# Four early weight pieces issued from GpSimd, their cast and subtraction on ticks of their own, the fifth after the sparse stage

## The chip, the core and the metric

The kernel runs on one core of one Trainium2 chip. TensorE (PE) multiplies, VectorE (DVE), ScalarE (ACT) and GpSimd (POOL) do the elementwise work, SyncE (SP) issues most DMAs. The metric is the device time of one execution in microseconds; lower is better. Before the change it is 521.82 us, the median of three runs from 516.04 to 524.46 us. Two per cent of that is 10.4 us.

## What is computed

Block-sparse attention over 4 batches, 8 heads, 768 positions and 64 dimensions (a position sees its neighbour blocks of 32, the first and the last block, and three sampled blocks; the first and last block see all), then a mixture of 8 experts with the best one chosen for each of 3072 tokens:

```python
scores = np.where(mask, scale * np.matmul(q, k.transpose(0, 1, 3, 2)), -1e9)
attn = softmax(scores); x = (attn @ v) as [3072, 512]
logits = x @ w_gate + modality_bias[modality_id]
e_idx = np.argmax(logits, axis=1)
for e in range(E):                       # 8 experts
    mask = e_idx == e
    h = np.maximum(x[mask] @ w1[e], 0.0)  # 512 x 1024
    out[mask] = gate_w[mask, None] * (h @ w2[e])  # 1024 x 512
```

## The kernel before

**Attention.** A list of items is worked off in one hand-written order for all engines (`manual_schedule`). An item of the sparse stage is a pair of query blocks, one of two batches; four items make a group m, 11 groups make a half, and two halves make groups 0 to 21. At each step t the loop runs the operations O, X, T, S, M, G, V, A, Y, W for items that lag behind t by fixed amounts. For a group: SP loads queries (L148), the values of its own sampled blocks (L525, six loads of 128 KB) and two more rows (L499, L500); POOL copies shared keys (L469, L473, L485) and shared values (L507); PE makes scores (L537), DVE masks them and takes the maximum (L545), ACT takes the exponent (L553), PE transposes (L562), ACT copies back (L567), PE weighs the values (L584 with the shared values, L593 with the group's own). Then the rows are turned (L600), gated (L610) and written to `x_d` (L335). Buffers for values alternate between two slots (`vbuf`, slots 7 and 8).

**Experts.** A group of experts is 256 tokens of one expert. Its weights come in 8 pieces of 512 KB: pieces 0 to 3 are `w1` (L720), 4 to 7 are `w2` (L724). A piece n is loaded into a staging buffer (`fetch`), cast to float32r by ACT (`split_high`, L731: the high part), and its remainder is taken by a subtraction (`split_low`, L737: the low part), on POOL in four quarters for the pieces in `POOL_SPLITS` (1, 2, 4, 7 ...), on DVE otherwise. A product then takes three matmuls: high by high, high by the low part of the tokens, low by high (L785 to L787 for the first layer `up`, L800 to L802 for the second, `down`). Between the layers ACT takes the relu (L792) and DVE the remainder (L793).

**The early groups.** Two expert groups are chosen before all tokens are routed. `choose` writes the expert's number to `grp_e` (L1061), and starts `early_groups`, which is stepped along with the last part of the sparse stage. Each of its ticks is one step t of the attention loop. `TICKS` and `load` decide what happens at a tick: at tick 0 pieces 0 and 1 are fetched; at tick 6 piece 0 is split and piece 2 fetched; at tick 9 piece 1 is split and piece 3 fetched; at tick 12 piece 2 is split and piece 4 fetched. `fetch` reads the expert's number from `grp_e` into a register of SP (L706) and issues the DMA on SP, in line with the value loads of the sparse stage. When the sparse stage has issued its last own-value matmuls (`tail[0]`), `load(10, 5)` splits pieces 3 and 4 and fetches up to piece 9, and the 96 matmuls of the first layer follow, bank by bank: four banks, each with four c and two f. After each bank comes its relu. The second layer calls `load` before each f from the table `DOWN0`.

The staging buffers of pieces 0 to 7 of the first group are 0, 1, 0, 1, 0, 1, 0, 2 of `stg`; 0 and 1 lie in slot 4, and 2, 3 and 4 lie in slot 7, which the sparse stage uses for values until group 20 is done.

Of the kernel before, what the change touches and what calls it, by code (L numbers as in the profile page):

```python
# [26 lines left out]
E = 8  # L27
# [52 lines left out]
EVAC_DVE = ()  # L80
POOL_SPLITS = (1, 2, 4, 7, 15, 16, 21)

TICKS = (6, 9, 12)
DOWN0 = ((9, 5), (9, 7), (14, 7), (12, 9), (13, 9), (13, 9), (17, 9), (15, 10))
UP1 = ((13, 8), (13, 14), (17, 15), (20, 15))
DOWN1 = ((16, 17), (17, 16), (17, 17), (23, 18), (21, 17), (23, 18), (23, 19), (22, 19))
# [3 lines left out]
def attention_moe(ctx, tc, kD, qD, qH, v0, v1, blocks, modality, w_gate, bias, w1, w2, out):  # L90
    nc = tc.nc
# [32 lines left out]
    with ExitStack() as actx:  # L124
# [5 lines left out]
        def bank():  # L130
            return psum.tile([P, 512], F32, name="bank")
# [525 lines left out]
        stg, wh, wl, xg, xh, xl, hh, hl, og, xq = [], [], [], [], [], [], [], [], [], []  # L657
# [42 lines left out]
        experts = {}  # L700
        out_t = dram_disjoint_views(out, 2)

        def expert(g):
            if g not in experts:
                src = grp_e[g] if g < NEAR else grp[:, g:g + 1]
                experts[g] = nc.sync.value_load(src[0:1, :], min_val=0, max_val=E - 1)  # L706
            return experts[g]

        def staged(n):
            return stg[(0, 1, 0, 1, 0, 1, 0, 2)[n] if n < 8 else n % NSTG]  # L710

        def fetch(n):
            g, c = divmod(n, 8)
            e = expert(g)
            if c < 4:
                if g < FIRST_Q:
                    src = w1[bass.ds(e, 1), c * P:(c + 1) * P, :].rearrange("e p f -> p (e f)")
                else:
                    src = w1[bass.ds(e, 1)].rearrange("e (p c) f -> c p (e f)", c=4)[c]
                nc.sync.dma_start(staged(n), src)  # L720
            else:
                c -= 4
                src = w2[bass.ds(e, 1), 2 * c * P:(2 * c + 2) * P, :].rearrange("e (k p) f -> p (e k) f", p=P)
                nc.sync.dma_start(staged(n).rearrange("p (k f) -> p k f", k=2), src)  # L724

        def split(n):
            split_high(n)
# [2 lines left out]
        def split_high(n):  # L730
            nc.scalar.copy(wh[n % NRING], staged(n))  # L731
# [49 lines left out]
        def up(g, c, f, o):  # L781
            h, l = wh[(8 * g + c) % NRING], wl[(8 * g + c) % NRING]
            o = o[:, (f % 2) * GT:(f % 2 + 1) * GT]
            fs = slice(f * P, (f + 1) * P)
            nc.tensor.matmul(o, lhsT=h[:, fs], rhs=xh[g % 2][:, c, :], start=c == 0 and f % 2 == 0, stop=False)  # L785
            nc.tensor.matmul(o, lhsT=h[:, fs], rhs=xl[g % 2][:, c, :], start=False, stop=False)  # L786
            nc.tensor.matmul(o, lhsT=l[:, fs], rhs=xh[g % 2][:, c, :], start=False, stop=c == 3 and f % 2 == 1)  # L787

        def relu(k, o):
            rh = hh[0][:, 2 * k:2 * k + 2, :].rearrange("p a b -> p (a b)")  # L790
            rl = hl[k // 2][:, k % 2 * 2:k % 2 * 2 + 2, :].rearrange("p a b -> p (a b)")
            nc.scalar.activation(rh, o, AF.Relu)  # L792
            nc.vector.scalar_tensor_tensor(rl, o, 0.0, rh.bitcast(F32), ALU.max, ALU.subtract)  # L793
# [22 lines left out]
        def early_groups():  # L816
            now = {"fetch": 0, "split": 0, "gather": 0, "column": 0}

            def load(nf, ns):
                while True:  # L820
                    f, p = now["fetch"], now["split"]
                    if p < ns and p < f:
                        split(p)
                        now["split"] += 1
                    elif f < nf and f - NSTG < p and (f < 8 * NEAR or known):
                        fetch(f)
                        now["fetch"] += 1
                    else:
                        return

            def rows(g):
                if now["gather"] == g and ready[g] and (g != 1 or tail[1]):
                    if g == 1:
                        expert_slots(8)
                    gather(g)
                    now["gather"] += 1

            def columns(g):
                for n in range(2):
                    if now["column"] == 2 * g + n and now["gather"] > g:  # L840
                        column(g, n, bank())
                        now["column"] += 1
                        return

            expert_slots(0)
            tick, wait = 0, 0
            while not tail[0]:
                rows(0)
                if now["gather"]:
                    wait += 1  # L850
                    if wait > 4:
                        columns(0)
                p = sum(tick >= x for x in TICKS)
                load(p + 2, p)
                tick += 1
                yield "tick"
            expert_slots(2, 5, 6, 7)
            while now["column"] < 2:
                rows(0)
                columns(0)  # L860
            load(10, 5)
            for k in range(4):
                o = bank()
                for c in range(4):
                    for f in (2 * k, 2 * k + 1):
                        up(0, c, f, o)
                    rows(1)
                    yield
                relu(k, o)
            o = [bank() for _ in range(2)]  # L870
            for f in range(8):
                load(*DOWN0[f])
                for t in range(2):
                    down(0, f, t, o[t])
                    rows(1)
                    yield
                if f in (3, 7):
                    columns(1)
            while not tail[1]:
                yield  # L880
            rows(1)
            for t in range(2):
                give(0, t, o[t])
            while now["column"] < 4:
                columns(1)
            o = [bank() for _ in range(4)]
            for c in range(4):
                load(*UP1[c])
                for f in range(8):
                    up(1, c, f, o[f // 2])  # L890
                    if f % 2:
                        rows(2)
                        yield
            for k in range(4):
                relu(k, o[k])
            o = [bank() for _ in range(2)]
            for f in range(8):
                load(*DOWN1[f])
                for t in range(2):
                    down(1, f, t, o[t])  # L900
                    rows(2)
                    yield
                if f in (5, 6):
                    columns(2)
            for t in range(2):
                give(1, t, o[t])
            while not ready[2]:
                yield
            rows(2)
            load(22, 17)  # L910
            while now["column"] < 6:
                columns(2)
            piece_numbers(bank())
            load(22, 20)
# [537 lines left out]
```

## Time and profile before

| | |
|---|---|
| median of 3 runs | 521.82 us (516.04 to 524.46) |
| the profiled execution | 518.86 us, span of its instructions 517.2 us |
| granted TensorE clock, mean | 0.994 |
| PE busy | 495.8 us (96%) |
| DVE, ACT, POOL busy | 389.9, 339.1, 296.1 us |
| DMA moved | 119.40 MB, 231 GB/s |

The profile is one execution. Times in its views are us from the start of the span. The busy share of an engine over the whole span is a mean over stages with different limits: the dense and sparse attention (to about 227 us), the two early expert groups, and the other expert groups. A row of waits names who ended the waiting; "issue" stands where no semaphore did. A row of the timeline gives start, duration, engine, line, operation and tiles of one instruction or of a merged row of equal ones, and in brackets the engine's idle time before it.

### The profile page before, as it was taken

What the parts mean: (1) busy time and instruction counts of PE and PEld (TensorE: products, weight loads), DVE (VectorE), ACT (ScalarE), POOL (GpSimd) and SP (SyncE); (2) the same over time, 40 slices, a digit from 0 to 9 for tenths busy, and PEclk for the clock granted to TensorE, in tenths of its full rate; (3) what the DMA queues carried; (4) which work ended last, traced back from release to release, by engine and by line L of the source; (5) the groups of instructions that cost most, each with busy time, mean ns of one, the idle gap of its engine ahead of it and who ended that gap; (6) DMA issues with size and microseconds to landing.
All of it is one profiled execution on the core that took longest, in us unless ns stands there. A gap on an engine that the chain in (4) does not pass through costs nothing.

```text
span 517.2 us, 18866 instructions
## 1 busy us (share of the span) xinstructions
PE 495.8 (96%) x7170; PEld 418.6 (81%) x7170; DVE 389.9 (75%) x1127; ACT 339.1 (66%) x777; POOL 296.1 (57%) x530
## 2 busy tenths in 40 slices
PE   7999899999999999699999999999999999999994
PEld 5677677777778776599888898989989899898983
DVE  7996598687689899686976669586785867759572
ACT  3799877988989988654554456464564546646471
POOL 3579675676458876733457724573845648465410
PEclk9999999999999999999999999999999999999998
DMA  7997888868945768947857974867859567595750
GB/s 275 329 246 203 247 245 248 248 202 238 255 158 164 209 194 254 273 144 248 281 202 263 325 275 146 301 202 247 271 168 323 179 245 264 178 313 180 267 203 23
DMA packets 49699, 119.40 MB, mean 231 GB/s; under 512 B 8513, under 2 KB 8897, under 8 KB 49601
## 3 DMA queue, kind: packets, MB, share of 16 engines
q1 hardware_dynamic: 44656, 105.00, 64.3%
q0 software_dynamic: 4944, 13.11, 6.9%
q8 instruction: 58, 0.95, 0.8%
q14 instruction: 41, 0.33, 0.2%
HBM read 105.50 MB, written 12.85 MB: 229 GB/s over the span
## 4 chain that ended last, share of the span: by engine, by line
PE 54%; DMA 13%; DVE 11%; issue 8%; POOL 7%; SPq 3%; POOLq 2%; ACT 1%; DVEq 0%; ACTq 0%
PE bank L537 6%; POOL slot L757 6%; PE bank L562 6%; DMA slot<-x_d,gq 6%; PE bank L802 4%; PE bank L785 4%; PE bank L801 4%; PE bank L800 4%; PE bank L787 4%; PE bank L786 4%; DMA out<-slot,si 4%; PE bank L584 3%; PE bank L593 3%; PE bank L438 2%; PE bank L610 2%
## 5 line engine op out<-in xcount | busy, mean ns | idle before, releaser
L737 DVE TENSOR_TENSOR slot<-slot 128x1024 fp32r<-128x1024 f32 x97 | 116.6, 1231 | 43.0 <-ACT slot L731 33.3
L757 POOL DMA_INDIRECT slot<-x_d,gq x72 | 92.1, 1279 | 76.6 <-DVE slot L764 57.2
L731 ACT CAST slot<-slot 128x1024 fp32r<-128x1024 f32 x104 | 106.2, 1047 | 44.1 <-PE bank L786 16.9
L785 PE MATMUL bank<-slot 128*128 128x256 f32 x384 | 107.2, 279 | 0.0
L786 PE MATMUL bank<-slot 128*128 128x256 f32 x384 | 106.3, 277 | 0.0
L787 PE MATMUL bank<-slot 128*128 128x256 f32 x384 | 106.3, 277 | 0.0
L553 ACT ACTIVATE a<-y,mn 128x256 f32<-128x256 f32 x176 | 88.7, 513 | 4.0 <-DVE mn L545 3.8
L802 PE MATMUL bank<-slot 128*128 128x512 f32 x200 | 79.1, 396 | 0.2
L800 PE MATMUL bank<-slot 128*128 128x512 f32 x200 | 78.4, 392 | 0.0
L801 PE MATMUL bank<-slot 128*128 128x512 f32 x200 | 78.4, 392 | 0.0
L786 PEld LDWEIGHTS bank<-slot 128*128 128x128 f32 x384 | 72.3, 188 | 0.4
L785 PEld LDWEIGHTS bank<-slot 128*128 128x128 f32 x384 | 72.1, 188 | 0.6
L787 PEld LDWEIGHTS bank<-slot 128*128 128x128 f32 x384 | 72.1, 188 | 0.0
L545 DVE CUSTOM_DVE_ANT_1 y<-bank,smask 128x256 f32<-128x256 f32 x176 | 66.1, 416 | 0.3
L485 POOL COPY slot<-slot 128x128 f32 x264 | 64.2, 293 | 0.0
L507 POOL TENSOR_SCALAR slot<-slot 32x1024 f32<-32x1024 f32 x40 | 41.8, 1046 | 25.3 <-issue 9.3
L567 ACT COPY at<-bank 128x512 f32<-128x512 f32 x88 | 50.7, 578 | 6.9 <-PE bank L562 6.7
L562 PE MATMUL bank<-ident,a 128*128 128x128 f32 x352 | 52.3, 282 | 0.5 <-ACT a L409 0.5
L792 ACT ACTIVATE slot<-bank 128x512 fp32r<-128x512 f32 x48 | 27.1, 598 | 36.6 <-PE bank L787 35.4
L537 PE MATMUL bank<-slot,q_raw 64*32 64x256 f32 x1408 | 49.2, 382 | 0.0
L793 DVE SCALAR_TENSOR_TENSOR slot<-bank,slot 128x512 fp32r<-128x512 f32 x48 | 30.4, 684 | 21.9 <-ACT slot L792 21.7
L802 PEld LDWEIGHTS bank<-slot 128*128 128x128 f32 x200 | 37.6, 188 | 8.9 <-DVE slot L793 1.1
(301 smaller groups left out, 865.4 us busy)
## 6 DMA issues: line engine op xcount, KB each, us to landing
slot<-w SPq DMA_DIRECT2D x105, 512.0 KB
slot<-v SPq DMA_DIRECT2D x180, 128.0 KB
q_raw<-qH SPq DMA_DIRECT2D x22, 256.0 KB
x_d<-xr SPq DMA_DIRECT2D x22, 256.0 KB
slot<-v SPq DMA_DIRECT2D x16, 256.0 KB
slot<-kD SPq DMA_DIRECT2D x13, 256.0 KB
slot<-v SPq DMA_DIRECT2D x4, 768.0 KB
slot<-kD SPq DMA_DIRECT2D x3, 768.0 KB
```

The lines of the kernel that those rows point to most:

```text
L537: nc.tensor.matmul(sp[u][32 * pr:32 * pr + 32, b * 256:(b + 1) * 256], lhsT=q[r, b * NPAIR + pr, n, :], rhs=kv[r, s0:s0 + 8, b, pr, :], st ...
L553: nc.scalar.activation(a[:, u, :], y[:, u, :], AF.Exp, bias=mn[:, u:u + 1], scale=-1.0, accum_out=total[:, u:u + 1])
L562: nc.tensor.transpose(tp[:, k:k + P], a[:, u, c * P:(c + 1) * P], ident)
L731: nc.scalar.copy(wh[n % NRING], staged(n))
L737: eng.tensor_tensor(l[:, k:k + size], staged(n)[:, k:k + size], h[:, k:k + size].bitcast(F32), ALU.subtract)
L757: nc.gpsimd.indirect_dma_start(out=xq[0][:, 4 * t + k, :], out_offset=None, in_=table, in_offset=bass.IndirectOffsetOnAxis(ap=gq[:, k, 2 * ...
L785: nc.tensor.matmul(o, lhsT=h[:, fs], rhs=xh[g % 2][:, c, :], start=c == 0 and f % 2 == 0, stop=False)
L786: nc.tensor.matmul(o, lhsT=h[:, fs], rhs=xl[g % 2][:, c, :], start=False, stop=False)
L787: nc.tensor.matmul(o, lhsT=l[:, fs], rhs=xh[g % 2][:, c, :], start=False, stop=c == 3 and f % 2 == 1)
L800: nc.tensor.matmul(o, lhsT=hh[0][:, f, ts_], rhs=h[:, fs], start=f == 0, stop=False)
L801: nc.tensor.matmul(o, lhsT=hh[0][:, f, ts_], rhs=l[:, fs], start=False, stop=False)
L802: nc.tensor.matmul(o, lhsT=hl[f // 4][:, f % 4, ts_], rhs=h[:, fs], start=False, stop=f == 7)
```

## The change

`TICKS` is replaced by `SOON`, a table of ticks and tokens: f is a fetch, h a `split_high`, l a `split_low`. The fetches of pieces 0 to 3 go to `nc.gpsimd`, which reads the expert's number itself. Piece 4 is no longer fetched in the sparse stage; `load(9, 4)` behind it splits piece 3 and fetches pieces 4 to 8 on SP. The buffers of pieces 4 to 7 become 4, 0, 1, 2. The first layer runs two banks at a time with c outside, so that 48 matmuls come before the first two relus; `load(10, 5)`, which splits piece 4, comes behind these.

```diff
-TICKS = (6, 9, 12)
+SOON = {1: 'f0 f1', 6: 'h0', 7: 'l0', 8: 'h1', 9: 'f2', 10: 'l1', 12: 'f3 h2', 13: 'l2'}
...
-            return stg[(0, 1, 0, 1, 0, 1, 0, 2)[n] if n < 8 else n % NSTG]
+            return stg[(0, 1, 0, 1, 4, 0, 1, 2)[n] if n < 8 else n % NSTG]
...
-                nc.sync.dma_start(staged(n), src)
+                eng.dma_start(staged(n), src)
...
+            def soon(what, n):
+                if what == "f":
+                    fetch(n, nc.gpsimd)
+                    now["fetch"] = n + 1
+                elif what == "h":
+                    split_high(n)
+                else:
+                    split_low(n, nc.gpsimd if n in POOL_SPLITS else nc.vector)
+                    now["split"] = n + 1
...
-                p = sum(tick >= x for x in TICKS)
-                load(p + 2, p)
+                for token in SOON.get(tick, "").split():
+                    soon(token[0], int(token[1]))
...
-            load(10, 5)
-            for k in range(4):
-                o = bank()
+            load(9, 4)
+            for k0 in (0, 2):
+                o = [bank() for _ in range(2)]
                 for c in range(4):
-                    for f in (2 * k, 2 * k + 1):
-                        up(0, c, f, o)
-                    rows(1)
-                    yield
-                relu(k, o)
+                    for k in range(2):
+                        for f in range(2):
+                            up(0, c, 2 * (k0 + k) + f, o[k])
+                        rows(1)
+                        yield
+                for k in range(2):
+                    relu(k0 + k, o[k])
+                load(10, 5)
```

The order of SP where pieces 0 and 1 were fetched, before the change (L500 loads values, L148 queries, L516 reads block numbers; the two L525 are the next value loads):

```order
L500 DMA slot<-v 32x1024
L148 DMA q_raw<-qH 128x512
L516 TENSOR_LOAD rb_i
L706 TENSOR_LOAD grp_e_76
L706 ISA x2
L720 ISA
L720 DMA slot<-w 128x1024
L720 ISA
L720 DMA slot<-w 128x1024
L525 ISA
L525 DMA slot<-v 32x1024
```

The L706 and L720 rows leave this place, and L525 follows L516; L706 stands on SP behind the last `x_d` rows now, with piece 4 (L724) as the first load after it. The same place on POOL, as a difference (L507 copies shared values, L469 and L473 shared keys):

```order
 L507 TENSOR_SCALAR slot<-slot 32x1024 x2
 L462 TENSOR_LOAD rb_i
+L706 TENSOR_LOAD grp_e_76
+L706 ISA x2
+L720 ISA
+L720 DMA slot<-w 128x1024
+L720 ISA
+L720 DMA slot<-w 128x1024
 L469 TENSOR_SCALAR slot<-slot 128x512
 L473 TENSOR_SCALAR slot<-slot 128x2x2x64 x2
```

The read of the expert's number and both issues now stand between the copies of shared values and those of shared keys. Two more such issues stand further on, one ahead of each of the next two subtractions. The third place is ACT behind the sparse stage (L731 are the casts of pieces, L792 the relus, L306 an exponent of the routing):

```order
-L731 CAST slot<-slot 128x1024 x2
-L330 ACTIVATE xr<-xr,gs 128x512
-L602 COPY xT<-bank 128x512
-L792 ACTIVATE slot<-bank 128x512 x3
+L731 CAST slot<-slot 128x1024
+L330 ACTIVATE xr<-xr,gs 128x512
+L602 COPY xT<-bank 128x512
+L792 ACTIVATE slot<-bank 128x512 x2
+L731 CAST slot<-slot 128x1024
 L306 ACTIVATE exps_88<-dl 128x2x8
-L792 ACTIVATE slot<-bank 128x512
+L792 ACTIVATE slot<-bank 128x512 x2
```

The cast of piece 4 moves behind the first two relus, and the last two relus now stand together.

## Rows read from the trace of the kernel before

**Rows 1.** Page, part 1: busy us, share of the span, instructions of each engine.

```profile
PE 495.8 (96%) x7170; PEld 418.6 (81%) x7170; DVE 389.9 (75%) x1127; ACT 339.1 (66%) x777; POOL 296.1 (57%) x530
```

**Rows 2.** Busy time by stretches, end of the sparse stage and start of experts.

```profile
core 0: us, PE busy (x) PEld busy (x) DVE busy (x) ACT busy (x) POOL busy (x), PEclk, DMA share, GB/s
...
199.00:204.00 5.00, 3.90 (x121) 2.77 (x128) 4.81 (x25) 3.44 (x11) 2.82 (x2) 1.00 0.64 164
204.00:214.60 10.60, 9.08 (x246) 7.13 (x246) 10.20 (x48) 10.29 (x31) 6.28 (x8) 1.00 0.94 298
214.60:217.10 2.50, 0.02 (x2) 0.00 (x0) 0.45 (x4) 0.53 (x2) 2.41 (x4) 1.00 0.88 208
217.20:220.60 3.40, 3.40 (x20) 3.28 (x21) 1.12 (x3) 1.53 (x4) 1.05 (x2) 0.51 0.93 277
220.60:227.30 6.70, 6.40 (x231) 5.71 (x229) 4.69 (x36) 3.57 (x11) 0.81 (x1) 1.00 0.56 166
227.30:241.00 13.70, 13.70 (x151) 13.31 (x144) 9.90 (x38) 4.83 (x9) 6.80 (x7) 1.00 0.58 197
```

**Rows 3.** Waits of the engines, 199 to 227.3 us: total us, times, longest.

```profile
DVE slot L779 <- ACT slot L778: 4.4, 1, 4.4
...
PE bank L593 <- DMA slot<-v: 2.4, 3, 1.3
```

**Rows 4.** Waits of SP's queue, 165 to 235 us.

```profile
SPq L500 <- DMA slot<-w: 4.9, 2, 2.5
```

**Rows 5.** Chain of waits, 196 to 228 us: start, us, what.

```profile
214.62 2.49 issue
...
217.72 1.90 PE bank L774 x8
```

**Rows 6.** DMA queues, first 207 to 214.2 us, then 214.2 to 215.6: packets, MB, share.

```profile
q1 hardware_dynamic: 722, 2.13, 92.9%
...
q8 instruction: 1, 0.02, 5.6%
```

**Rows 7.** Timeline of POOL: start, us, instruction, idle before and its releaser.

```profile
192.02 0.64 POOL L469 TENSOR_SCALAR slot<-slot 128x512 f32<-128x512 f32 x1 [1.62 <-PE bank L577]
...
198.84 2.01 POOL L742 DMA_INDIRECT slot<-x_d,gi_e  x1 [0.18 <-POOL slot L507]
201.16 0.96 POOL L742 DMA_INDIRECT slot<-x_d,gi_e  x1 [0.30 <-issue]
206.41 2.83 POOL L737 TENSOR_TENSOR slot<-slot 128x256 fp32r<-128x256 f32 x4 [4.29 <-ACT slot L731]
...
213.31 2.78 POOL L737 TENSOR_TENSOR slot<-slot 128x256 fp32r<-128x256 f32 x4 [1.75 <-ACT slot L731]
...
229.06 3.94 POOL L737 TENSOR_TENSOR slot<-slot 128x256 fp32r<-128x256 f32 x4 [5.54 <-ACT slot L731]
```

**Rows 8.** Timeline of ACT, 224 to 262 us: the second relu, casts behind the last.

```profile
234.37 0.60 ACT L792 ACTIVATE slot<-bank 128x512 fp32r<-128x512 f32 x1 [1.60 <-PE bank L787]
...
241.34 3.88 ACT L731 CAST slot<-slot 128x1024 fp32r<-128x1024 f32 x4
```

**Rows 9.** Timeline of DVE: subtraction of piece 0, of pieces 5 and 6.

```profile
198.59 1.21 DVE L737 TENSOR_TENSOR slot<-slot 128x1024 fp32r<-128x1024 f32 x1
...
242.45 2.35 DVE L737 TENSOR_TENSOR slot<-slot 128x1024 fp32r<-128x1024 f32 x2
```

**Rows 10.** Timeline of PE: scores of group 21, values of group 20, two low-part matmuls.

```profile
203.93 1.09 PE L537 MATMUL bank<-slot,q_raw 64*32 64x256 f32 x32
...
213.22 0.31 PE L584 MATMUL bank<-slot,at 128*64 128x64 f32 x2
...
241.11 0.39 PE L801 MATMUL bank<-slot 128*128 128x512 f32 x1
...
243.87 0.39 PE L801 MATMUL bank<-slot 128*128 128x512 f32 x1
```

**Rows 11.** Timeline of SP, 195 to 262 us: issue of piece 4.

```profile
216.71 0.41 SPq L724 DMA_DIRECT2D slot<-w  x1
```

More of the change, by code (lines that the diff above doesn't have):

```diff
@@ L701, in attention_moe, with expert, fetch @@
         out_t = dram_disjoint_views(out, 2)
-        def expert(g):
-            if g not in experts:
+        def expert(g, eng):
+            if (g, eng) not in experts:
                 src = grp_e[g] if g < NEAR else grp[:, g:g + 1]
-                experts[g] = nc.sync.value_load(src[0:1, :], min_val=0, max_val=E - 1)
-            return experts[g]
+                experts[g, eng] = eng.value_load(src[0:1, :], min_val=0, max_val=E - 1)
+            return experts[g, eng]
         def staged(n):
-            return stg[(0, 1, 0, 1, 0, 1, 0, 2)[n] if n < 8 else n % NSTG]
-        def fetch(n):
+            return stg[(0, 1, 0, 1, 4, 0, 1, 2)[n] if n < 8 else n % NSTG]
+        def fetch(n, eng=nc.sync):
             g, c = divmod(n, 8)
-            e = expert(g)
+            e = expert(g, eng)
             if c < 4:
@@ L723, in fetch @@
                 src = w2[bass.ds(e, 1), 2 * c * P:(2 * c + 2) * P, :].rearrange("e (k p) f -> p (e k) f", p=P)
-                nc.sync.dma_start(staged(n).rearrange("p (k f) -> p k f", k=2), src)
+                eng.dma_start(staged(n).rearrange("p (k f) -> p k f", k=2), src)
         def split(n):
```

## The prediction

> **What bounds the kernel now.** Part 1 of the page comes first: PE is busy 495.8 of 517.2 us [rows 1], so 21 us is the most that any change to waiting can give, and this one touches only the end of the sparse stage. Next come the busy times of stretches [rows 2]. From 227.3 us on PE is full (13.70 of 13.70 us): the expert groups run at PE's pace, and what is gained or lost ahead of them reaches the end one for one, unless a new wait arises there. [...] From 199 to 214.6 us PE is idle 1.1 + 1.5 us, but DVE is busy 4.81 of 5.00 and 10.20 of 10.60 us, and ACT 10.29 of 10.60: the elementwise engines are the limit. [...]
>
> "Issue" means that no semaphore held PE; it stopped within a run of equal matmuls. The DMA view shows what it lacked: from 207 to 214.2 us, 2.13 MB of weights and values went through and no packet of instructions; the packet of queue 8 stands in 214.2 to 215.6 [rows 6]. [...] I read the gap as a late refill behind full DMA engines (busy share 0.94 from 204 on [rows 2]).
>
> **The change, part by part.**
>
> *SP without pieces 0 to 4.* SP's queue waited 4.9 us, in two waits of up to 2.5 us, on value loads (L500) for a weight load to land [rows 4], though the two have no data in common. Without weight loads in SP's line those waits go, and value loads are issued up to 4.9 us earlier, into a stretch where the DMA share is 0.64 (199 to 204 us [rows 2]). The fifth piece, issued at 216.71 [rows 11], leaves the crowded stretch.
> - PE's waits for values, 2.4 us in three [rows 3], should go. What they are worth is bounded by the idle time of DVE in the same stretches, 0.19 + 0.40 us [rows 2]: between 0 and 0.6 us. I take 0, since DVE keeps all its instructions.
> - The gap at 214.62: if the value loads have been served earlier and piece 4 is away, the refill comes in time. Worth 2.5 us, at least 0. I take 2.5.
> - The low clock follows from the gap: 3.4 us at 0.51 do the work of 1.7 us. Worth 1.7 us, or 0 if the gap stays. I take 1.7.
>
> *Four issues on POOL.* No row shows POOL issuing a plain load; the nearest are its gathers of 128 rows, 0.96 to 2.01 us each [rows 7]. Four cost 3.8 to 8.0 us of POOL. What hides them is its idle time at these very places: 1.62 us ahead of L469 for pieces 0 and 1, 4.29 us ahead of the first subtraction for piece 2, 1.75 us ahead of the second for piece 3 [rows 7]. Pieces 0 and 1 can be up to 2.4 us too long; behind them wait the key copies, which end before the gather at 198.84 [rows 7] and are read by the scores of group 21 at 203.93 [rows 10]: 5.1 us of room. Piece 3 can be 0.3 us too long. Cost 0, bounds 0 and 0.3.
>
> The long gather (2.01 us) began at 198.84, during a 1.21 us subtraction of DVE from 198.59 [rows 9]; the one after it took 0.96. [...]
>
> *Ticks.* The cast of piece 1 moves ahead of one copy on ACT, the subtraction of piece 0 some instructions back on DVE. Both engines keep their work: 0.
>
> *Piece 4 behind the first 48 matmuls.* Before, its subtraction on POOL ended at 233.0 (229.06 + 3.94 [rows 7]). Now the cast stands behind two relus. The second bank's relu started at 234.37 [rows 8], as 48 matmuls were done; the new order needs the same 48, then relus at 234.4 and 234.9, a cast at 235.4 of 0.97 us (3.88 over four [rows 8]), then POOL for 2.8 to 3.9 us [rows 7]: 239.2 to 240.3. The first matmul that reads it is at 241.11 [rows 10]: 0.8 us of room at worst. Cost 0, bounds 0 and 0.5.
>
> *The last two relus together.* The casts of pieces 5 onwards start about 0.5 us later than 241.34, the subtraction of piece 5 then not at 242.45 but at 243.0, and ends (1.18 us each [rows 9]) at 244.1; PE reads it at 243.87 [rows 10]. Cost 0.3 us, bounds 0 and 0.7.
>
> *Five pieces to load after the stage instead of four.* The DMA share is 0.56 to 0.58 there [rows 2], and the stages ahead of it move nothing that PE lacks: 0.
>
> **Sum.** 518.86 − 2.5 − 1.7 + 0.3 = 514.96 us for the profiled execution, 3.9 us less. That execution lies 2.96 us under the median of the runs, 521.82; the runs spread from 516.04 to 524.46. On the median the forecast is **517.9 us**.
>
> **Rivals.**
> 1. *The gap stays, or another opens.* The bytes are nearly the same, and pieces now compete from a second queue with eight value loads in flight. For it: the engines were at 0.94 for 10 us, and only one piece in five leaves. Against: the hole at 199 to 204 takes up loads. Then −0.6 to +0.5: about 521.8 us. [...]
> 2. *Value waits were on the path too.* PE's 2.4 us count as well, if DVE's and ACT's work closes up when PE is early: 2.4 + 2.5 + 1.7 = 6.6 us, **515.2 us**. Against it stands the full DVE.
> 3. *Slower: POOL's issues are held up.* Place: pieces 2 and 3 ahead of the subtractions. If DVE's running keeps each issue for as long as DVE is busy (4.81 us in a 5 us stretch) and the two are 5 us each, they overrun the idle 4.29 and 1.75 by 0.7 and 3.25 us; value copies (L507) and so PE's L584 (213.22 [rows 10]) come up to 4 us late. With no gain elsewhere 525.8 us, with the gain 521.9; about 524. It decides once an issue lasts over 4.3 us; the longest like it is 2.01.
>
> **Chances and range.** The forecast (gap and low clock go) 0.55; the gap stays 0.22; all of PE's waits count 0.10; POOL slows it 0.13. The likeliest gives 517.9. Low end: the lowest run shown less the largest sum of my terms, 2.5 + 1.7 + 0.6 − 0.3 = 4.5, so 516.04 − 4.5 = 511.5. High end: the median plus 1.7, 523.5, which takes in the second case and the lower half of the slower one. For the forecast alone 515 to 520. Two per cent, about what a measurement of this kernel can tell from no change, is 10.4 us: under 511.4 or over 532.3. No case of mine reaches either without the spread of the runs. Faster 0.04, same 0.93, slower 0.03.
>
> **What would show it.** In the profile after: SP's L500 no longer waits for slot<-w; the stretch that answers to 199 to 204 us has a higher DMA share; no "issue" gap of over 1 us and no clock at half ahead of the first L785, which starts near 223 and not at 227.3; POOL's plain loads at 1 to 2 us; the subtraction of piece 4 ends before the first L801. Wrong would be: PE stopping again without a semaphore, DVE idle where it is now full, or a wait of the first `down` matmuls for POOL.

## The result and the profile after

The kernel after takes 521.63 us, the median of 22 runs (517.83 to 526.96); the kernel before, run beside it, 517.31 us, also over 22 runs (515.25 to 525.02). The ratio is 1.0053, 95% interval [1.0029, 1.0076]: about half a per cent slower, where 0.75% faster was forecast. (The ratio, here and below, compares only the runs within 1.5% of the fastest of their kernel, so it is not that of the two medians.) The 521.82 us shown ahead was a median of three; nineteen more runs moved it by 4.5 us. The time lies within the forecast range, 511.5 to 523.5, but only by luck: the range was built on that high median. Built on 517.31 in the same way, its high end would be 519.0 (517.31 + 1.7).

The profiled execution of after took 522.37 us, span 520.8. PE, DVE, ACT and POOL are busy as before [rows 1]:

```profile
PE 497.7 (96%) x7170; PEld 419.4 (81%) x7170; DVE 389.3 (75%) x1127; ACT 341.3 (66%) x777; POOL 299.2 (57%) x534
```

POOL at the end of the sparse stage (columns as in [rows 7]; L720 issues a piece, L469 copies shared keys, L737 subtracts, L507 copies shared values):

```profile
189.19 1.36 POOL L720 DMA_DIRECT2D slot<-w  x2 [3.48 <-DVE xr L447]
190.56 0.65 POOL L469 TENSOR_SCALAR slot<-slot 128x512 f32<-128x512 f32 x1
...
197.03 0.61 POOL L469 TENSOR_SCALAR slot<-slot 128x512 f32<-128x512 f32 x1
...
207.03 0.58 POOL L720 DMA_DIRECT2D slot<-w  x1 [1.07 <-DVE slot L737]
209.29 2.79 POOL L737 TENSOR_TENSOR slot<-slot 128x256 fp32r<-128x256 f32 x4 [1.68 <-ACT slot L731]
212.17 2.16 POOL L507 TENSOR_SCALAR slot<-slot 32x1024 f32<-32x1024 f32 x2
214.29 0.60 POOL L720 DMA_DIRECT2D slot<-w  x1
```

An issue takes only 0.58 to 0.78 us (the 0.78 is f1_later's). But POOL stands idle for 3.48 us ahead of the first two, and the key copies of group 20 wait behind them. In the kernel before they came after 1.05 us, at 183.84, about 1 us before the expert's number was written (its L1061 is L1074 of after):

```profile
183.84 0.62 POOL L469 TENSOR_SCALAR slot<-slot 128x512 f32<-128x512 f32 x1 [1.05 <-PE bank L577]
184.68 0.15 DVE L1061 TENSOR_SCALAR grp_e<-cm 128x1 int32<-128x1 f32 x1
```

What POOL lacked in after is the expert's number, which its read (L706) takes from `grp_e`. The timeline of DVE in after has the write:

```profile
187.60 0.15 DVE L1074 TENSOR_SCALAR grp_e<-cm 128x1 int32<-128x1 f32 x1
188.29 0.69 DVE L447 TENSOR_TENSOR xr<-bank,rt 128x512 f32<-128x512 f32 x1
```

POOL was free from 185.71 (189.19 − 3.48), the number was written at 187.75 (187.60 + 0.15), and the rest up to 189.19, 1.44 us, lies in instructions without a busy time in this view, the read among them. The row names L447, which ends at 188.98, but pool_wait_only below shows that POOL need not wait for it.

PE's timeline of after, at two early stops, at the wait for ACT and at the first layer of the experts:

```profile
190.71 0.29 PE L610 MATMUL bank<-wg_raw,xT 128*64 128x8 f32 x5 [0.60 <-issue]
...
194.49 0.74 PE L593 MATMUL bank<-slot,at 128*32 128x64 f32 x38
197.19 0.85 PE L593 MATMUL bank<-slot,at 128*32 128x64 f32 x26 [1.96 <-issue]
...
219.99 1.15 PE L584 MATMUL bank<-slot,at 128*64 128x64 f32 x30 [1.87 <-ACT at L567]
...
230.80 0.39 PE L785 MATMUL bank<-slot 128*128 128x256 f32 x1
```

The 2.49 us of [rows 5] is gone, but 1.96 us of "issue" stand inside L593, and 1.87 us of waiting for ACT at L584. The busy times of stretches show the clock behind each (answering [rows 2]; 195.20 to 197.20 and 218.10 to 220.00 are the idle pieces):

```profile
185.00:190.70 5.70, 5.12 (x160) 3.53 (x159) 5.44 (x29) 5.12 (x17) 2.21 (x4) 1.00 0.81 239
190.70:195.20 4.50, 4.49 (x127) 3.58 (x126) 4.29 (x26) 3.41 (x13) 4.42 (x16) 1.00 1.02 346
195.20:197.20 2.00, 0.04 (x5) 0.01 (x2) 1.24 (x3) 2.00 (x6) 1.92 (x3) 1.00 1.03 258
197.40:200.90 3.50, 3.50 (x66) 2.79 (x63) 2.78 (x8) 1.35 (x4) 3.50 (x14) 0.51 0.45 113
...
218.10:220.00 1.90, 0.03 (x3) 0.01 (x2) 1.83 (x9) 1.90 (x5) 0.40 (x1) 1.00 0.96 257
221.30:224.80 3.50, 3.50 (x23) 3.43 (x22) 2.15 (x5) 2.64 (x9) 3.17 (x4) 0.51 0.64 218
...
230.80:244.50 13.70, 13.70 (x149) 13.34 (x144) 8.99 (x38) 5.08 (x9) 6.10 (x7) 1.00 0.69 225
```

So there are two stretches at a granted clock of 0.51, 3.5 us each, where the execution of before had one, of 3.4 us [rows 2]. From the first L785, 3.5 us later than before, PE is full again, and the end comes 3.6 us later: nothing was lost in the experts. Not all of the 3.5 us belongs to the change, though: this execution was already 2.9 us behind at the key copies of group 19 (179.27 against 176.35), ahead of the first moved issue. One pair of traces can't size half a per cent; the runs below do.

### The profile page after: what moved, and what is told of

It reads as the page before. It is cut to its first block, busy times and chain, and to the rows that moved or that the text cites. A ratio compares the mean times of both kernels' runs of the same rounds, so it can differ in the third digit from the quotient of the medians.

```text
span 520.8 us, 18877 instructions
## 1 busy us (share of the span) xinstructions
PE 497.7 (96%) x7170; PEld 419.4 (81%) x7170; DVE 389.3 (75%) x1127; ACT 341.3 (66%) x777; POOL 299.2 (57%) x534
## 4 chain that ended last, share of the span: by engine, by line
PE 59%; DMA 13%; DVE 9%; issue 7%; POOL 6%; SPq 2%; ACT 2%; POOLq 1%; DVEq 0%; ACTq 0%
PE bank L537 7%; PE bank L562 6%; PE bank L785 6%; PE bank L786 6%; PE bank L787 6%; DMA slot<-x_d,gq 5%; POOL slot L757 5%; PE bank L802 4%; PE bank L801 4%; PE bank L800 4%; PE bank L593 3%; PE bank L584 3%; DMA out<-slot,si 3%; PE bank L610 2%; DMA slot<-kD 2%
## 5 line engine op out<-in xcount | busy, mean ns | idle before, releaser
L737 DVE TENSOR_TENSOR slot<-slot 128x1024 fp32r<-128x1024 f32 x97 | 116.2, 1226 | 44.6 <-ACT slot L731 44.5
L757 POOL DMA_INDIRECT slot<-x_d,gq x72 | 95.2, 1322 | 76.9 <-DVE slot L764 57.6
L731 ACT CAST slot<-slot 128x1024 fp32r<-128x1024 f32 x104 | 106.3, 1047 | 41.2 <-PE bank L786 30.3
L785 PE MATMUL bank<-slot 128*128 128x256 f32 x384 | 107.0, 279 | 0.0
L786 PE MATMUL bank<-slot 128*128 128x256 f32 x384 | 106.2, 277 | 0.0
L801 PE MATMUL bank<-slot 128*128 128x512 f32 x200 | 78.4, 392 | 0.0
L800 PE MATMUL bank<-slot 128*128 128x512 f32 x200 | 78.4, 392 | 0.0
L785 PEld LDWEIGHTS bank<-slot 128*128 128x128 f32 x384 | 72.1, 188 | 0.6
L786 PEld LDWEIGHTS bank<-slot 128*128 128x128 f32 x384 | 72.2, 188 | 0.4
L485 POOL COPY slot<-slot 128x128 f32 x264 | 64.2, 292 | 0.0
L507 POOL TENSOR_SCALAR slot<-slot 32x1024 f32<-32x1024 f32 x40 | 41.7, 1044 | 28.5 <-issue 10.7
L567 ACT COPY at<-bank 128x512 f32<-128x512 f32 x88 | 50.7, 577 | 11.0 <-PE bank L562 10.7
L792 ACT ACTIVATE slot<-bank 128x512 fp32r<-128x512 f32 x48 | 28.7, 598 | 29.6 <-PE bank L787 26.7
L793 DVE SCALAR_TENSOR_TENSOR slot<-bank,slot 128x512 fp32r<-128x512 f32 x48 | 32.2, 689 | 17.1 <-ACT slot L792 17.1
```

The lines of the kernel that those rows point to most:

```text
L737: eng.tensor_tensor(l[:, k:k + size], staged(n)[:, k:k + size], h[:, k:k + size].bitcast(F32), ALU.subtract)
L757: nc.gpsimd.indirect_dma_start(out=xq[0][:, 4 * t + k, :], out_offset=None, in_=table, in_offset=bass.IndirectOffsetOnAxis(ap=gq[:, k, 2 * ...
L800: nc.tensor.matmul(o, lhsT=hh[0][:, f, ts_], rhs=h[:, fs], start=f == 0, stop=False)
L801: nc.tensor.matmul(o, lhsT=hh[0][:, f, ts_], rhs=l[:, fs], start=False, stop=False)
```

## The experiments

Fifteen kernels ran (two of them repeats), each beside runs of the kernel before on the same chip. The table gathers them by one property of the trace: whether POOL stands still for the expert's number ahead of the key copies of group 20. "Copies" is the time from the key copies of group 19 to those of group 20 in the trace, 7.5 us in the kernel before; "clock" is the mean granted clock of the compared runs, 0.9944 to 0.9947 for the kernel before in each comparison that has it.

| kernel | number read by POOL | copies, us | ratio to before | clock |
|---|---|---|---|---|
| after | tick 1 | 11.3 | 1.0053 [1.0029, 1.0076] | 0.9923 |
| after_again | tick 1 | 11.9 | 1.0063 [1.0026, 1.0099] | 0.9906 |
| pool_only | first tick | 11.8 | 1.0131 [1.0083, 1.0178] | 0.9882 |
| old_first_layer | tick 1 | 11.4 | 1.0087 [1.0046, 1.0128] | 0.9896 |
| pool_wait_only | tick 1, no load | 9.3 | 1.0064 [1.0026, 1.0102] | 0.9876 |
| f1_later | tick 1 | 10.7 | 1.0052 [1.0017, 1.0086] | 0.9912 |
| cast_later | tick 1 | 11.3 | 1.0069 [1.0025, 1.0112] | 0.9905 |
| sp_issue | not | 7.5 | 1.0012 [0.9980, 1.0045] | 0.9946 |
| new_first_layer | not | 7.5 | 1.0030 [0.9993, 1.0066] | 0.9946 |
| sp_cast_later | not | 7.5 | 1.0027 [0.9992, 1.0062] | 0.9930 |
| sp_cast_tick14 | not | 7.5 | 1.0025 [0.9994, 1.0056] | 0.9925 |
| f01_sp | tick 9 | 7.5 | 1.0013 [0.9974, 1.0051] | 0.9935 |
| read_tick3 | tick 3, no load | 7.5 | 0.9991 [0.9958, 1.0025] | 0.9952 |
| only01_tick3 | tick 3 | 7.5 | 1.0014 [0.9974, 1.0053] | 0.9932 |
| f01_tick3 | tick 3 | 7.5 | 1.0053 [1.0015, 1.0090] | 0.9909 |
| f01_tick3_again | tick 3 | 7.5 | 0.9999 [0.9967, 1.0031] | 0.9927 |

### Which part costs

The first four undo or do one part each.

**sp_issue**: the change, with SP issuing.

```diff
                 if what == "f":
-                    fetch(n, nc.gpsimd)
+                    fetch(n)
```

> The changed kernel with one part undone: pieces 0 to 3 are issued by SP again; ticks, buffers, the fifth piece and the new order of the first layer stay as changed. Theory P (the loss comes from the issue on POOL: pieces run beside the value loads instead of in line with them): the time falls back to that of before, ratio 0.998 to 1.002. Theory U (the loss comes from what was moved behind the sparse stage: casts of piece 4 and 5 behind the relus, the fifth load): still 1.004 to 1.007. Theory T (the loss comes from the ticks: piece 2 fetched three ticks later, so its cast and the copies behind it on ACT are late): still 1.004 to 1.007.

Measured 520.34 us, ratio 1.0012. Without POOL's issues no loss is left that can be told from noise, though the ticks, the buffers and the new first layer are all there. The interval, [0.9980, 1.0045], still overlaps with that of after, [1.0029, 1.0076]; the pairs below part the two more clearly.

**pool_only**: the kernel before, with only the issue of pieces 0 to 3 moved to POOL.

```diff
+            eng = nc.gpsimd if n < 4 else nc.sync
+            e = expert(g, eng)
...
-                nc.sync.dma_start(staged(n), src)
+                eng.dma_start(staged(n), src)
```

> The kernel before with one part of the change alone: pieces 0 to 3 are issued by POOL at the old ticks, piece 4 by SP as before. Theory P: 1.004 to 1.007, with SP's waits on weight loads gone. Theories U and T: 0.998 to 1.002.

Measured 526.9 us over six runs, 1.0131: the largest loss of all, and above the 1.004 to 1.007 expected. POOL's timeline shows two waits, and PE's shows who pays (in this file L721 and L738 are the lines L720 and L737 of before):

```profile
188.48 1.36 POOL L721 DMA_DIRECT2D slot<-w  x2 [3.96 <-DVE mn L545]
...
201.98 0.60 POOL L721 DMA_DIRECT2D slot<-w  x1 [5.62 <-DVE slot L738]
202.60 0.64 POOL L469 TENSOR_SCALAR slot<-slot 128x512 f32<-128x512 f32 x1
```

```profile
209.11 1.15 PE L584 MATMUL bank<-slot,at 128*64 128x64 f32 x32 [0.98 <-POOL slot L507]
219.98 1.97 PE L584 MATMUL bank<-slot,at 128*64 128x64 f32 x32 [4.07 <-POOL slot L507]
```

The 5.62 us is a wait for a staging buffer: at the old ticks piece 2 is issued just behind the subtraction of piece 0 on DVE that frees it. The key copies of group 21, the value copies and so PE's L584 stand behind it. The new ticks are what spares the kernel after this second wait (1.07 us there).

**old_first_layer**: the change with the bank-by-bank first layer and the old `load(10, 5)` ahead of it.

```diff
-            load(9, 4)
-            for k0 in (0, 2):
-                o = [bank() for _ in range(2)]
+            load(10, 5)
+            for k in range(4):
+                o = bank()
```

> The changed kernel with the first layer bank by bank as before and piece 4 split ahead of it; piece 4 is still fetched behind the sparse stage. Theory U: most of the loss goes, 0.999 to 1.002, unless piece 4 arrives too late for the cast that now stands ahead of the first relu. Theories P and T: 1.004 to 1.007.

Measured 524.68 us, 1.0087: the loss stays, a little above the range expected. The same L593 as in after stops, at the same matmul, for 2.51 us, and 10.0 us at a granted clock of 0.50 follow:

```profile
190.40 0.74 PE L593 MATMUL bank<-slot,at 128*32 128x64 f32 x38
193.65 1.06 PE L593 MATMUL bank<-slot,at 128*32 128x64 f32 x26 [2.51 <-issue]
```

```profile
193.20:203.20 10.00, 9.45 (x140) 7.71 (x141) 9.81 (x44) 5.40 (x16) 8.22 (x19) 0.50 0.70 211
```

**new_first_layer**: the kernel before, with only the new first layer (in it a later load takes piece 4's buffer before the piece is split, so that piece's data is replaced; the work is the same).

> The kernel before with the new first layer alone (two banks at a time, piece 4 split behind the first two relus); issues and ticks as before. Theory U: 1.002 to 1.006, with PE waiting for the low parts of pieces 4 or 5 at the first second-layer matmuls. Theories P and T: 0.998 to 1.002.

Measured 522.05 us, 1.0030 [0.9993, 1.0066]. The number alone decides nothing: it lies in theory U's range and above that of P and T, and its interval holds both no change and the loss of after. But the wait that U foretold is missing: from the first L785 (226.17) through the first L800 and L801 (239.61 and 239.93) PE's timeline shows no wait. With old_first_layer, which undoes the new first layer and keeps the loss, and sp_issue, the loss comes with the issue on POOL.

### Why the issue on POOL costs

Two theories: POOL's line stands still behind its wait (W), or the first two loads, now earlier, stand ahead of PE's instructions (I).

**pool_wait_only** takes W alone: SP issues everything, POOL only reads the number at tick 1.

```diff
                 if what == "f":
-                    fetch(n, nc.gpsimd)
+                    fetch(n)
...
+                if tick == 1:
+                    expert(0, nc.gpsimd)
```

> The kernel after, but SP issues pieces 0 to 3 (as in sp_issue), and POOL only reads the expert's number at tick 1, at the place where it read it in the kernel after; it issues none of the four loads. Two theories on why the issue on POOL costs time. W: POOL's line stands still in its wait for the number (idle 3.48 us ahead of the loads of pieces 0 and 1), and all copies of keys and values behind it come late. I: not the wait but the early issue costs: pieces 0 and 1 start about 2 us earlier than from SP, 1 MB stands ahead of PE's next instructions, PE stops with issue in the middle of L593 (1.96 us at 195.23) and then runs 3.4 us at half its clock. W: the wait of 3 to 4 us on POOL is here too, and the time is that of the kernel after, 1.004 to 1.006 of before. I: pieces 0 and 1 are issued about where they were in sp_issue (191), no gap of over 1 us within L593 at 195, and the time is that of sp_issue, 0.999 to 1.003.

Measured 520.47 us, 1.0064: all of the loss, without one load on POOL. The profiled execution took 526.13 us, the longest of its twelve, so the sizes of its rows lie at the upper end. POOL is idle 2.85 us ahead of the key copies of group 20, where it was 1.05 in the kernel before, it has not caught up by the value copies of group 21 (202.13, 2.16 us), and PE waits for these. PE's L577, which releases the copies in the kernel before, had ended at 189.36. The copies start at 191.21, 0.81 us after the write of the number (190.25 + 0.15; L1076 is L1074 of after) and before L447 has ended (191.63), so it is the number that POOL waits for:

```profile
190.25 0.15 DVE L1076 TENSOR_SCALAR grp_e<-cm 128x1 int32<-128x1 f32 x1
190.94 0.69 DVE L447 TENSOR_TENSOR xr<-bank,rt 128x512 f32<-128x512 f32 x1
191.21 0.62 POOL L469 TENSOR_SCALAR slot<-slot 128x512 f32<-128x512 f32 x1 [2.85 <-PE bank L562]
...
202.13 2.16 POOL L507 TENSOR_SCALAR slot<-slot 32x1024 f32<-32x1024 f32 x2
```

```profile
201.79 1.09 PE L537 MATMUL bank<-slot,q_raw 64*32 64x256 f32 x30 [1.04 <-DVE rt L445]
...
205.03 1.98 PE L584 MATMUL bank<-slot,at 128*64 128x64 f32 x32 [1.37 <-POOL slot L507]
```

```profile
203.60:210.20 6.60, 5.23 (x63) 4.54 (x68) 6.38 (x38) 4.95 (x15) 2.83 (x3) 0.50 0.88 264
```

PE is idle for 1.04 us up to 201.79, waiting for DVE, and for 1.37 us up to 205.03, waiting for POOL. The clock of 0.50 begins at 203.5, about where the second piece begins, so that piece lies inside the slow stretch and didn't bring it on. The L584 of 32 matmuls takes 1.98 us, not the 1.15 of a full clock.

**read_tick3** is its counterpart: the same read two ticks later (`if tick == 3`), behind the key copies, when the number is there.

> As pool_wait_only (SP issues all loads, POOL only reads the expert's number), but at tick 3, behind the key copies of group 20, where the number has long been written and POOL does not wait. The runs so far show where the loss lies: pool_wait_only has a mean granted clock of 0.9876 over its runs against 0.9944 of the kernel before, which is 3.6 us more lost at the lower level of the clock, and 515.45 us without it, as the kernel before. Theory W (POOL's wait holds back the key copies of group 20, PE idles in longer pieces and falls to half its clock): here 0.999 to 1.003 and a mean clock of 0.993 to 0.995. Rival R (any reading on POOL in this stage costs, wait or not): 1.004 to 1.007 and a mean clock under 0.992.

Measured 519.23 us, 0.9991, and no idle time of POOL at the read (it begins the value copies 0.08 us after the key copies). A read on POOL that found the number cost nothing that can be told (0.9991); one that had to wait cost about half a per cent (1.0064). The intervals of the two, [1.0026, 1.0102] and [0.9958, 1.0025], just fail to touch; they ran on different chips, each against the kernel before beside it.

**f1_later** keeps the wait and moves piece 1 to tick 4.

```diff
-SOON = {1: 'f0 f1', 6: 'h0', ...
+SOON = {1: 'f0', 4: 'f1', 6: 'h0', ...
```

> The kernel after, but piece 1 is issued at tick 4 and not right behind piece 0 at tick 1. POOL's wait for the expert's number stays where it was, ahead of piece 0; only half of the early megabyte is in front of PE's instructions at 195 us. W: POOL's wait is the same, so 1.004 to 1.006 of before. I: the gap of 1.96 us within L593 at 195 is gone or under 1 us, with no half clock behind it, and the time falls by up to 1.96 + 1.7 us, to 0.998 to 1.002.

Measured 519.44 us, 1.0052. The stop within L593 shrank to 0.55 us, as I had it, and the loss stayed, as W had it; so the second early piece and the long stop are not what costs; pool_wait_only, which issues both from SP, loses as much.

**f01_sp**: pieces 0 and 1 on SP, 2 and 3 on POOL (`fetch(n, nc.sync if n < 2 else nc.gpsimd)`).

> The kernel after, but SP issues pieces 0 and 1 and POOL pieces 2 and 3. If the loss comes with the first two pieces (by W or by I): 0.999 to 1.003 of before, and the gap within L593 at 195 is gone. If it comes with pieces 2 and 3, whose issue on POOL pushed the second subtraction from 213.3 to behind 214.3: 1.004 to 1.006.

Measured 519.77 us, 1.0013 [0.9974, 1.0051]: the later two issues cost nothing that can be told.

**f01_tick3**: all four on POOL, the first two at tick 3 (`SOON = {3: 'f0 f1', ...`).

> The kernel after, but pieces 0 and 1 are issued by POOL at tick 3, two steps of the attention loop later: the number is then long written, and the key copies of group 20 stand ahead of them. W: POOL has no wait of over 1 us for the number, the copies come in time, 0.999 to 1.003 of before. I: the two loads start some 5 us later, the gap at 195 is gone, also 0.999 to 1.003, unless it opens at the next packet of instructions (some 4 to 5 us on) instead. If it stays at 1.004 to 1.006 with neither the wait nor the gap, the loss is that of pieces 2 and 3.

Measured 520.07 us, 1.0053: neither the wait nor a half clock ahead of the experts in the trace (its granted clock is 1.00 from 185 to 225 us, and the first L785 starts at 224.94), and yet the loss. (The trace is of the shortest of the twelve executions, 517.40 us; the mean clock of all, 0.9909, is as low as in kernels whose POOL waits.) This spoke against W, and three runs followed. **only01_tick3** has pieces 0 and 1 on POOL at tick 3 and the others on SP:

> Pieces 0 and 1 issued by POOL at tick 3 (no wait for the number), pieces 2 and 3 by SP. f01_tick3, with all four on POOL, came to 1.0053 and a mean clock of 0.9909 although POOL did not wait, which W does not give; f01_sp, with only pieces 2 and 3 on POOL, to 1.0013 and 0.9935. If two loads on POOL's own queue at this place cost by themselves (they compete with the value loads for the DMA engines, 1 MB in a stretch at a DMA share of 1.02): 1.004 to 1.006, clock 0.990 to 0.992. If only the wait costs (W), or only all four together: 0.999 to 1.003, clock 0.993 to 0.995.

Measured 519.54 us, 1.0014. **f01_tick3_again** and **after_again** ran on one chip:

> The kernel of f01_tick3 once more (all four loads on POOL, the first two at tick 3, where POOL does not wait for the number). It came to 1.0053 [1.0015, 1.0090] though its trace shows neither the wait nor a half clock ahead of the experts; with only the first two (only01_tick3) or only the last two (f01_sp) on POOL the time was that of the kernel before. If the wait is all that costs (W): 0.999 to 1.003, mean clock 0.993 to 0.995, and the first result was chance at the edge of its interval. If four loads on POOL cost together without any wait: 1.004 to 1.007 again, mean clock 0.990 to 0.992.

> The kernel after once more, on the same chip as f01_tick3_again, for a second trace and a direct comparison. W: 1.004 to 1.007 of before, mean clock 0.991 to 0.993, POOL's wait of 3 to 4 us ahead of the first two loads again, key copies of group 20 some 11 us behind those of group 19 (7.4 us in the kernel before), and a half clock ahead of the experts. W also gives f01_tick3_again 0.3 to 0.5 per cent less than this. If four loads on POOL cost by themselves, the two are equal.

Measured 519.93 us, 0.9999 [0.9967, 1.0031], against 521.73 us, 1.0063 [1.0026, 1.0099]. Their difference is that the two loads stand behind the key copies or ahead of them:

```profile
186.31 2.97 POOL L485 COPY slot<-slot 128x128 f32 x12
189.23 1.36 POOL L720 DMA_DIRECT2D slot<-w  x2
```

```profile
189.50 1.36 POOL L720 DMA_DIRECT2D slot<-w  x2 [4.04 <-DVE mn L545]
190.87 0.65 POOL L469 TENSOR_SCALAR slot<-slot 128x512 f32<-128x512 f32 x1
```

The first fence is f01_tick3_again, the second after_again. The two results of the tick 3 kernel overlap only from 1.0015 to 1.0031; I take the first as chance at its edge, since the direct comparison, only01_tick3 and f01_sp agree. That is a judgement over four results, not a proof: the clock of the repeat, 0.9927, lies between the range given for W (0.993 to 0.995) and that for a cost of the four loads together (0.990 to 0.992), and the two runs of this kernel together are no clear case of either.

The traces show where the time goes. From the key copies of group 19 to the first matmul of the experts (L785; L786 in pool_only's file), the seven kernels whose POOL waits take 50.7 to 53.6 us, 52.3 on average, and the nine others 48.2 to 51.4, 49.8 on average; before takes 51.0. From there to the end the two sets are alike, 290.8 us on average in both, if pool_only (295.0) is left out. So the loss arises in this stretch, and its 2.5 us are near the difference of the mean ratios, 1.0074 against 1.0018. The latter also leaves room for some 0.2% from the other parts of the change, which no run here tells from nothing.

### A wait that was worth nothing

PE's 1.87 us for L567 stand behind ACT's cast of piece 2 (1.04 us). **cast_later** puts that cast one tick on, behind both L567:

```diff
-SOON = {..., 12: 'f3 h2', 13: 'l2'}
+SOON = {..., 12: 'f3', 13: 'h2 l2'}
```

> The kernel after, but the cast and the subtraction of piece 2 come at tick 13 together, so that the 1.04 us cast stands behind the two L567 copies of its step and not ahead of them. In the kernel after PE waits 1.87 us for L567 at this cast and then runs 3.4 us at half its clock. If the loss is half clock behind PE's longer idle pieces (W and its clock): this gap falls to about 0.9 us, the mean clock rises by 0.001 to 0.003 over the kernel after (0.9923), and the ratio falls to 1.000 to 1.004, less than all of the loss, since the wait of POOL at tick 1 stays. If the gap costs nothing: 1.004 to 1.006.

**sp_cast_later** is the same on sp_issue.

> cast_later with all loads on SP's queue. sp_issue, which has the same 1.80 us wait of PE for L567 and a half clock behind it, came to 1.0012. If that wait costs by its half clock: 0.995 to 0.999, faster than the kernel before, with a mean clock of 0.995 to 0.996. If it costs nothing: 0.999 to 1.003.

Measured 1.0069 and 1.0027. The gain that both were run for did not come: cast_later lies above both of its ranges, and sp_cast_later in the range for a wait that costs nothing. The two differ only in who issues the four pieces and ran on one chip, so they are a second pair like after and sp_issue: mean times of 523.3 and 520.2 us, clocks of 0.9905 and 0.9930. The wait for L567 did fall to 0.93 us, and another of 1.64 us opened behind it. The row is from sp_cast_later; cast_later has the same 1.64 us at its L1111:

```profile
213.12 1.15 PE L584 MATMUL bank<-slot,at 128*64 128x64 f32 x30 [0.93 <-ACT at L567]
...
219.49 0.60 PE L1111 MATMUL bank<-hoh,lhs 128*128 128x2 f16 x18 [1.64 <-DVE hoh L1101]
```

The cast now stood ahead of ACT's second L778, which DVE needs. **sp_cast_tick14** moved it behind that too.

> sp_cast_later with the cast and subtraction of piece 2 one tick further on, behind both L778 copies: at tick 13 the cast stood ahead of the second L778, DVE got it late, and PE waited 1.64 us for what DVE makes of it (L1111). PE's wait for L567 (0.93 us there) stays that short. If these waits and the half clock behind them cost: 0.995 to 0.999 of before, faster than sp_issue (1.0012) and sp_cast_later (1.0027). If they lie beside the work of DVE and ACT: 0.999 to 1.003.

Measured 520.37 us, 1.0025: L1111 waited 0.75 us, and an L584 further on 1.93 us, for POOL's value copies. From 214 to 225 us DVE is busy 9.90 of 11.00 us, PE 7.54 and ACT 7.33: I read DVE as the limit here, and PE's idle time as only changing its place. No kernel of these beats the kernel before by more than its interval.

## Why the prediction failed, step by step

- **The step that failed: four issues on POOL, cost 0.** The issues themselves were sized too high (0.58 to 0.78 us each, not 0.96 to 2.01). What was left out is what an issue brings along: the read of `grp_e`, and with it a wait of POOL for DVE. The step says what hides the issues, "its idle time at these very places: 1.62 us ahead of L469", but that L469, at 192.02 [rows 7], belongs to group 21. The order put them ahead of the key copies of group 20, one group earlier, where the trace has 1.05 us and where the number is not yet written (it was at 184.83, with the copies at 183.84). What the runs showed in place of the cost of 0: a wait of 3.48 us, and about half a per cent, or 2.5 us, with it. The prediction asked how long POOL would be busy, and not when what it needs would be there. Rival 3 had the right engine and the wrong place and cause: it looked for a hold-up at pieces 2 and 3, which in f01_sp cost nothing that can be told.
- **The gap at 214.62, −2.5 us.** This step failed as well, without POOL's part in it: no run shows the term. That the gap is a late refill, a packet of instructions that PE waits for, was read off the packet beside it [rows 6]; no run shows more than that. In after PE no longer stops there, and nothing was won; nor in sp_issue, where POOL does not wait, and which at 1.0012 shows none of the 4.2 us of this term and the next. PE now reaches L584 earlier and waits 1.87 us for ACT, which was there before as well, hidden behind PE's own delay (0.18 us in that row of before). Rival 1, "the gap stays, or another opens", has what became of the stop right: it moved to L593. That its time, 521.8, meets the measured 521.63 is luck: it stands for no change from a median that was 4.5 us too high, and a change did come, from another cause.
- **The half clock, −1.7 us.** No run shows this term. In these traces a clock of 0.50 or 0.51 stands near idle pieces of PE, wherever they lie (3.4 us of it near the 2.49 us in before, 3.5 us near the 1.96 us in after and 3.5 us near the 1.87 us there), but not near every one: f01_tick3 has the same wait of 1.88 us for L567, and its granted clock is 1.00 from 185 to 225 us. So taking the gap away did not give the clock back. The execution of after has two such stretches, not none, and its mean clock over the runs is lower. By an estimate that takes PE to have work all the time, in pool_wait_only this is the whole loss: its mean time of 521.9 us at a clock of 0.9876 gives away 6.5 us (521.9 × 0.0124), the kernel before beside it 2.9 us (518.3 × 0.0055); the difference, 3.6 us, is that of the two mean times. In after_again it is 2.0 of 3.2 us, but in the first f01_tick3, where POOL does not wait, also 1.9 of 2.1: a lower clock is what the lost time looks like, and doesn't by itself tell the cause.
- **SP without pieces 0 to 4.** Right: the two L500 waits for weights [rows 4] are gone. Instead SP now waits 12.0 us, six times, at L499 until PE's L593 is through with the slot. That the 2.4 us of PE's waits for values were worth 0 was taken without a run to show it, and none isolates it: sp_issue, which keeps 1.0 us of that L500 wait, shows no loss, and no kernel shows a gain.
- **Ticks, cost 0; piece 4; the last two relus.** Right in sum as far as can be told: sp_issue, with all three, is at 1.0012 [0.9980, 1.0045]. Piece 4's subtraction ended at 242.24 (239.44 + 2.80), 238.8 on the scale of before, against 239.2 to 240.3 worked out; the 0.3 us for piece 5 did not appear (245.89, which is 242.4 on the scale of before, against 242.45 there).
- **The long gather, 2.01 us, during a subtraction of DVE** [rows 7], [rows 9]. Had DVE's running kept POOL's issues in the same way, as rival 3 supposes, the four would have been long. Here two issues at 189.19 took 1.36 us together, with DVE busy for 1.33 us of it: the rows do not show it for these loads.
- **The scale.** 3.9 us were taken from a median of three runs that lay 4.5 us above that of 22. The forecast's own time for the profiled execution, 514.96, would have been a worse guess still.

What stays open is the way from POOL's wait to the end. In four of the seven kernels whose POOL waits PE then waits at L584 for a late POOL copy: pool_wait_only (1.37 us) and pool_only (0.98 and 4.07) for L507, f1_later (1.30) and cast_later (0.84) for L485. In the two traces of after no engine but POOL itself waits for a POOL copy, and PE's idle pieces of over 0.12 us between 185 and 232 us come to 5.9 and 5.5 us, in that of before to 6.3. What differs there is DVE. Two of its instructions take longer, first in after, then in before:

```profile
194.97 1.20 DVE L332 TENSOR_SCALAR xr<-xr,gs 128x512 f32<-128x512 f32 x1
199.37 1.41 DVE L571 TENSOR_TENSOR rexp<-sums,quad 128x32 f32<-128x32 f32 x1
```

```profile
192.77 0.53 DVE L332 TENSOR_SCALAR xr<-xr,gs 128x512 f32<-128x512 f32 x1
194.99 0.26 DVE L571 TENSOR_TENSOR rexp<-sums,quad 128x32 f32<-128x32 f32 x1
```

Together the two take 1.20 to 3.30 us in the seven kernels whose POOL waits and 0.78 to 0.99 in before and the nine others. From the key copies of group 19 to the first L785, DVE's 211 instructions take 43.35 us in after and 44.40 in after_again, 42.31 in before. Why they take longer no run isolates: in after L332 runs beside POOL's L507 and in before beside L473, but L571 runs beside L485 in both. That the wait costs is shown by the pairs; that it reaches the end of after by way of DVE is not.

## What to carry to other kernels

When a DMA moves to another engine's queue, cost its operands first: the register it reads and the buffer it fills may be waits that the old queue could afford and the new one can't, because other engines' work stands in line behind them (here 3.48 us for the register in after, 5.62 us for the buffer in pool_only). Ask of each moved issue when what it needs is written, and put it behind the work that doesn't depend on that; two ticks were enough here to end the wait. And a stop of the bound engine in one profiled execution is no gain to be had until other work is shown to let it run on.

## What the runs showed of the hardware

**PE's stops without a semaphore came at fixed places.** Counted from the first matmul of each trace, those of over 0.6 us that stand as "issue" between 180 and 228 us are at matmuls 4379, 4506, 4632, 4885 and 5011 (126 or 127 apart, or twice that), in whichever kernel; which of them are long changes from run to run. L593 stopped behind its 38th matmul in after and old_first_layer alike (rows above). Here is L584 behind its 23rd, in f01_tick3_again and in after_again:

```profile
197.26 0.91 PE L584 MATMUL bank<-slot,at 128*64 128x64 f32 x23
200.74 0.46 PE L584 MATMUL bank<-slot,at 128*64 128x64 f32 x9 [2.57 <-issue]
```

```profile
199.22 0.91 PE L584 MATMUL bank<-slot,at 128*64 128x64 f32 x23
200.49 0.46 PE L584 MATMUL bank<-slot,at 128*64 128x64 f32 x9 [0.37 <-issue]
```

With its loads one matmul is two instructions (7170 of each [rows 1]), so the places are some 253 instructions apart. The pages of before and after have 58 packets of instructions on queue 8, and PE's 14,340 instructions come to 247 for each of these, near that distance; an estimate, since no row says which engine a packet was for. The time lost is not the same each time: 2.57 and 0.37 us at one place. The queues in the 4.9 us ahead of and into the stop of after show what the packet shared the engines with:

```profile
q0 software_dynamic: 288, 1.05, 62.4%
q1 hardware_dynamic: 264, 0.59, 39.2%
q8 instruction: 1, 0.02, 1.3%
```

That is 190.7 to 195.6 us: the DMA engines were full (the three rows add up to 102.9%), with the two pieces as the larger part. f1_later, with one piece there, stopped for 0.55 us at this place, after_again, with both, for 0.97, and sp_issue not at all.
